# Two more attention units turned by DMA transposes on a shared ring, and the mixed tiles' scores on quarters of the array

## The chip, the core and the metric

One NeuronCore of a Trainium2 chip runs the whole program in one launch. The metric is device time in microseconds, the median of the runs. The engines are TensorE (PE; its weight loads are PEld), VectorE (DVE), ScalarE (ACT), GpSimd (POOL) and SyncE (SP), whose queue issues most of the DMAs.

## What is computed

Attention over 4 batches, 8 heads, 576 positions and a head dimension of 64, with a bias from a small network on relative positions, and then a gated product over the 2304 tokens it yields (width 512, inner width 1536):

```python
scores = 0.125 * q @ k.T + bias[None]          # bias: relu(x @ w1 + b1) @ w2, x = log1p|i-j| / log1p(max(i,1))
p = exp(scores - max(scores)); p = p / (sum(p) + 1e-9)
x = (p @ v).transpose(0, 2, 1, 3).reshape(2304, 512)
out = ((x @ w_a) * (x @ w_b)) @ w_out
```

## The kernel before

The work is 32 units `u`: for each half `c` of the query rows (`c` = 0: rows 0 to 255 of each head; `c` = 1: the other 320), each of 4 batches and each of 4 pairs of heads. A unit of the first half has four tiles of 128 query rows (`A0 B0 A1 B1`: head A or B of the pair, row block), a unit of the second half five: `A2 B2 A3 B3` and the mixed tile `T`, which holds the last 64 rows of both heads, head A in partitions 0 to 63 and head B in 64 to 127. The 144 tiles are numbered by `n`; units 0 to 15 hold tiles 0 to 63 (`N0` = 16 a batch), units 16 to 31 tiles 64 to 143 (`N1` = 20 a batch).

`attn_steps` runs a loop over `n`. In step `n` the bias rows of tile `n+2` are loaded on SP's queue; `soft1(n)` lets DVE add scores and bias and take the row extremum (L508) and ACT take the exponential with its sum (L513); loads and preparation of coming units follow; then PE computes the scores of tile `n+1` (`qk`); and `soft2(n-1)` normalises tile `n-1`. What happens to a normalised tile depends on `NF` = 12:

- Units below `NF`: POOL scales in float32 (L563), a step later `turn` lets PE transpose the tile in five blocks (L575) and ACT copies them out of PSUM (L585); `pv` multiplies float32 values: 5 blocks by 2 heads.
- Units from `NF` on: `split_turn` makes a high half on POOL (L543) and a low half with two DVE instructions (L545), both float16, in one tile `ph`, and one DMA transpose on SP's queue turns it into `pt` (L551). `pv` multiplies 14 products by 2 heads in float16, with V split in two halves by ACT and DVE in `prep_v` (L439, L440). Their `pv` comes one step later than that of the units before.

Rings: the exponentials `p` have 3 buffers; `ph` has 2 in the pool `yp`, and 2 more in the pool of the second half for odd tiles beyond 64. PSUM has one buffer `qk` for scores and one buffer `tp` for the turned blocks; from tile 51 on, odd tiles' scores use `tp`, so that scores have two buffers. V of units below `NF` is loaded into the `vs` ring, V of the others into the ring `rv` of 2, which `v_scale` (the size of the next batch's V, begun at tiles 12, 28 and 38) uses as well.

Scores of units from 8 on use q and k each split in two float32r halves (`prep_k`, `prep_q`). An ordinary tile takes 4 products; `T` takes 8, with a tile `qt` of q's last 64 columns of both heads, padded by zeros from POOL (L422) and filled by ACT and DVE (L426, L427).

PE's order is written by hand: `merge` deals out steps of the gated product (`moe_main`, lines 702 to 758), of the weights' conversion and of the attention in fixed proportions; `LEADS` says how many tiles into the next batch a batch's product begins. The other engines are ordered by a scheduler. At the start `first_units` computes 16 units of the bias table through a ring `bo` of 6, each written to DRAM from POOL's queue (L174); the other 20 follow between tiles 48 and 61.

Of the kernel before, what the change touches and what calls it, by code (L numbers as in the profile page):

```python
# [47 lines left out]
NF = 3 * NP  # L48
# [4 lines left out]
def attention_moe(ctx, tc, q0d, q1d, kd, vd, idn, wp, wa, wb, wo, lsw, lg, rl, out):  # L53
# [10 lines left out]
    xt, cpool, epool, xpool, ypool = [], [None], [None], [None], [None]  # L64
# [210 lines left out]
    w16, wos, gpool = {}, {}, [None]  # L275
# [93 lines left out]
    def load_unit(u):  # L369
        b, hp, c = UNITS[u]  # L370
        n = TOK + TAIL * c
# [18 lines left out]
        else:  # L390
            rk = att.tile([128, S], F32, tag="rk", name="rk", bufs=1)
            rq = att.tile([128, 2, n], F32, tag="rq", name="rq", bufs=1)
            with paced():
                nc.sync.dma_start(out=rk, in_=kd[b, hp])
                nc.sync.dma_start(out=rq, in_=(q1d if c else q0d)[b, hp])
# [15 lines left out]
    def prep_q(u):  # L411
        b, hp, c = UNITS[u]
        rq = st["raw", u][1]
        if u < 2 * NP:
            st["qs", u] = rq
            return
        dst = att.tile([128, 2, 2 * TOK], F32R, tag="qs", name="qs", bufs=2)
        segs = [(dst.rearrange("p c (h n) -> p c h n", h=2), rq[:, :, 0:TOK])]
        if c:

            qt = xpool[0].tile([128, 2, 4, TAIL], F32R, tag="qt", name="qt", bufs=2)
            nc.gpsimd.memset(qt[:, :, 1:3].bitcast(F32), 0.0)  # L422
            segs.append((qt[:, :, ::3], rq[:, :, TOK:]))
            st["qt", u] = qt.rearrange("p c (h x) n -> p c h (x n)", h=2)
        for d, s in segs:
            nc.scalar.copy(d[:, 0], s)  # L426
            nc.vector.tensor_tensor(out=d[:, 1], in0=s, in1=d[:, 0].bitcast(F32), op=ALU.subtract)  # L427
        st["qs", u] = dst
# [31 lines left out]
    def qk(n):  # L460
        u, t = TILES[n]
        pool, tag = (tpp, "tp") if n > 3 * N0 + 2 and n % 2 else (qkp, "qk")
        ps = pool.tile([128, 2, 512], F32, tag=tag, name="qk", bufs=1)
        q, k = st["qs", u], st["ks", u]
# [7 lines left out]
        elif t == "T":  # L472
            prods = [(st["qt", u][:, p, j], k[:, j]) for p in range(2) for j in range(2)]
        else:
            j = int(t[0] == "B")
            c0 = TOK * j + 128 * (int(t[1]) % 2)
            prods = [(q[:, p, c0:c0 + 128], k[:, j]) for p in range(2)]
# [59 lines left out]
    def split_turn(n, p, rc):  # L537
# [3 lines left out]
        pool = cpool[0] if n > B * N0 and n % 2 else ypool[0]  # L541
        ph = pool.tile([128, 2 * S], F16, tag="ph", name="ph", bufs=2)
# [82 lines left out]
    def attn_steps():  # L625
        vgen = [None]
        for n in range(NT + 4):
# [11 lines left out]
            for ahead, un in ((a, TILES[n + a][0]) for a in (6, 4, 3, 1, 0) if n + a < NT and FIRST[TILES[n + a][0]] == n + a):  # L639
# [11 lines left out]
                elif ahead == int(un < NF):  # L651
# [16 lines left out]
            if n >= 3 * N0 + 4 and (n - 3 >= NT or TILES[n - 4][0] != TILES[n - 3][0]):  # L668
                pv(TILES[n - 4][0], pvp)
            if n == B * N0 + 1:  # L670
                chunk_pool(1)
            if n >= 2 and n - 2 < 3 * N0:
# [6 lines left out]
            elif N0 + 3 <= n < 3 * N0 + 3 and TILES[n - 3][0] != TILES[n - 2][0]:  # L679
# [8 lines left out]
    def moe_block(xs, rows, mps, vi, spill=False):  # L688
# [7 lines left out]
        for f in range(FC):  # L696
# [20 lines left out]
            else:  # L717
                gs.append(g_parts(g))
# [84 lines left out]
    LEADS = [3, 4, 4, 5] + [8] * 4  # L803
# [11 lines left out]
    with tc.tile_pool(name="bg", bufs=1, side="right") as bg, tc.tile_pool(name="eq", bufs=1, space=PSUM) as eq, \  # L815
# [21 lines left out]
        def first_units(banks):  # L837
            for un in range(NU0):
# [3 lines left out]
                bias_unit(bh, lambda: banks(un), un, hs, 6, nc.gpsimd)  # L842
# [63 lines left out]
    wstack.close()  # L906
    with tc.tile_pool(name="bg2", bufs=1, reuse_waits="tile") as bg:
# [5 lines left out]
        ypool[0] = ctx.enter_context(tc.tile_pool(name="yp", bufs=1, side="right", reuse_waits="tile"))  # L913
# [66 lines left out]
```

## Time and profile before

| | |
|---|---|
| Time, median of 3 runs | 760.75 us (758.56 to 760.82) |
| The profiled execution: its time, its span | 758.25 us, 756.4 us |
| PE busy, PEld busy | 703.1 us (93%), 541.8 us (72%) |
| DVE, ACT, POOL busy | 506.8 us (67%), 448.5 us (59%), 338.3 us (45%) |
| HBM read, written | 96.44 MB, 17.18 MB |
[...]

The profile gives busy time and share of the span for each engine, the costliest groups of instructions with what ended the idle time before them, and the DMA issues with their time to landing. A busy PE is not PE at its peak: matmuls are pipelined, so in a timeline the distance from one block's start to the next one's is what a block costs. The stages by tile: the reduction of tile 0 starts at 36.5 us, of tile 40 at 195.2, of tile 48 at 235.4, of tile 64 at 332.4, of tile 143 at 625.7; after that only the products remain.

### The profile page before, as it was taken

The page shows a single profiled execution, that of the slowest core. Times are in us where ns is not written, and L with a number is a line of the kernel's source. Part 1 is how long each engine was busy: PE and PEld are TensorE (multiplying, and loading weights), DVE is VectorE, ACT ScalarE, POOL GpSimd, SP SyncE. Part 2 cuts the span into 40 slices and gives each one's busy share as a digit, 9 for nine tenths or more (in the row PEclk, how much of TensorE's full clock was granted, in tenths as well). Part 3 has the DMA queues.
Part 4 walks back from the last instruction along what each step waited for, and adds up shares of the span by engine and source line. Part 5 has one row for each costly group of instructions (what it writes and reads, how often), then busy time and mean ns, then how long its engine had stood idle before and what let it go on. Part 6 is the DMA issues. An engine that isn't in the chain of part 4 may idle for free.

```text
span 756.4 us, 15529 instructions
## 1 busy us (share of the span) xinstructions
PE 703.1 (93%) x5451; PEld 541.8 (72%) x5451; DVE 506.8 (67%) x1220; ACT 448.5 (59%) x1021; POOL 338.3 (45%) x493
## 2 busy tenths in 40 slices
PE   6777898899899999998999999999999999999997
PEld 1245465678776565687877788788878877888886
DVE  7777688859986588666898888878987762110100
ACT  6878787878866687744655656556644553321310
POOL 3337667856773133223655445535543543411200
PEclk9999999999999999999999999999999999999999
DMA  8999676587745888888999999899899954000001
GB/s 257 315 367 297 221 227 201 160 263 254 257 120 149 222 188 187 212 184 195 214 265 214 248 243 210 200 263 241 202 210 253 178 119 126 11 1 29 2 14 42
DMA packets 167154, 142.96 MB, mean 189 GB/s; under 512 B 120228, under 2 KB 125092, under 8 KB 167076
## 3 DMA queue, kind: packets, MB, share of 16 engines
q1 hardware_dynamic: 159920, 126.20, 64.1%
q10 hardware_dynamic: 5876, 10.93, 5.2%
q0 software_dynamic: 1280, 4.84, 1.9%
q8 instruction: 43, 0.70, 0.4%
q14 instruction: 35, 0.29, 0.1%
HBM read 96.44 MB, written 17.18 MB: 150 GB/s over the span
## 4 chain that ended last, share of the span: by engine, by line
PE 33%; DVE 22%; issue 16%; ACT 11%; POOL 9%; DMA 7%; SPq 0%; DVEq 0%; POOLq 0%; ACTq 0%
PE ab L702 12%; PE o L751 10%; DVE p L508 5%; DVE ph L545 4%; POOL ph L543 4%; DMA bias<-bias_d 4%; ACT p L513 3%; PE psta L153 3%; POOL gl L727 2%; DVE ks L408 2%; PE pv L603 2%; DMA pt<-ph 2%; PE qk L480 2%; DVE wt L270 1%; DVE qs L427 1%
## 5 line engine op out<-in xcount | busy, mean ns | idle before, releaser
L702 PEld LDWEIGHTS <-w16t 128*128 128x128 f16 x2592 | 247.5, 98 | 47.7 <-issue 15.8
L702 PE MATMUL ab<-x,w16t 128*128 128x256 f16 x2304 | 271.1, 274 | 4.1 <-DVE g L712 2.0
L513 ACT ACTIVATE p<-p,mn 128x576 f32<-128x576 f32 x144 | 111.7, 776 | 138.6 <-DVE mn L508 127.6
L727 POOL TENSOR_TENSOR gl<-g,gh 128x256 fp32r<-128x256 f32 x96 | 79.4, 827 | 93.6 <-ACT gh L726 91.9
L751 PE MATMUL o<-wos,gh 128*128 128x512 f32 x384 | 120.8, 395 | 0.0
L557 POOL TENSOR_SCALAR sm<-sm 128x1 f32<-128x1 f32 x144 | 42.2, 293 | 168.5 <-ACT p L513 164.3
L545 DVE SCALAR_TENSOR_TENSOR ph<-p,sm,ph 128x64 f16<-128x64 f32 x192 | 100.3, 562 | 22.8 <-POOL ph L543 22.1
L508 DVE CUSTOM_DVE_ANT_0 p<-qk,bias 128x576 f32<-128x576 f32 x144 | 107.3, 748 | 12.0 <-PE tp L575 4.1
L543 POOL TENSOR_SCALAR ph<-p,sm 128x576 f16<-128x576 f32 x96 | 82.4, 858 | 49.4 <-DVE sm L558 37.4
L712 DVE SCALAR_TENSOR_TENSOR g<-ab,wv,asb 128x256 f32<-128x256 f32 x84 | 40.2, 479 | 71.5 <-ACT asb L710 71.2
L480 PE MATMUL qk<-ks,qs 128*128 128x288 f32 x384 | 73.0, 312 | 13.8 <-DVE mn L508 13.8
L751 PEld LDWEIGHTS o<-wos,gh 128*128 128x128 f32 x384 | 69.4, 188 | 16.3 <-issue 3.3
L480 PEld LDWEIGHTS qk<-ks,qs 128*128 128x128 f32 x384 | 55.8, 188 | 27.4 <-DVE mn L508 18.7
L751 PE MATMUL o<-wos,gl 128*128 128x512 f32 x192 | 75.0, 391 | 0.0
L726 ACT CAST gh<-g 128x256 fp32r<-128x256 f32 x96 | 38.4, 400 | 34.6 <-DVE g L712 34.4
L563 POOL TENSOR_SCALAR p<-p,sm 128x576 f32<-128x576 f32 x48 | 44.5, 927 | 26.6 <-DVE sm L558 18.3
L710 ACT ACTIVATE asb<-ab,wv 128x256 f32<-128x256 f32 x84 | 39.4, 469 | 28.3 <-PE ab L702 28.0
L558 DVE RECIPROCAL sm<-sm 128x1 f32<-128x1 f32 x144 | 23.0, 160 | 47.0 <-POOL sm L557 44.8
L408 DVE TENSOR_TENSOR ks<-rk,ks 64x576 fp32r<-64x576 f32 x48 | 45.8, 954 | 5.7 <-ACT ks L407 4.1
L751 PEld LDWEIGHTS o<-wos,gl 128*128 128x128 f32 x192 | 36.0, 188 | 7.9
L575 PE MATMUL tp<-idn,p 128*128 128x128 f32 x240 | 36.0, 281 | 5.0 <-ACT ptf L580 3.6
L603 PE MATMUL pv<-pt,vs 128*64 128x320 f16 (+1 forms) x560 | 40.4, 295 | 0.0
(105 smaller groups left out, 986.2 us busy)
## 6 DMA issues: line engine op xcount, KB each, us to landing
bias<-bias_d SPq DMA_DIRECT2D x128, 288.0 KB, 3.7
rv<-vd SPq DMA_DIRECT2D x32, 320.0 KB, 3.9
rk<-kd SPq DMA_DIRECT2D x24, 288.0 KB, 3.3
wraw<-wa SPq DMA_DIRECT2D x12, 512.0 KB, 6.6
wraw<-wb SPq DMA_DIRECT2D x12, 512.0 KB, 5.5
wraw<-wo SPq DMA_DIRECT2D x12, 512.0 KB, 4.3
bias_d<-bo ACTq DMA_DIRECT2D x20, 295.5 KB, 3.7
rq<-q1d SPq DMA_DIRECT2D x16, 320.0 KB, 4.1
```

The costliest lines, as they stand in the source:

```text
L408: nc.vector.tensor_tensor(out=ks[ol, j], in0=rk[sl], in1=ks[sl, j].bitcast(F32), op=ALU.subtract)
L480: nc.tensor.matmul(ps[:, hf, :HB], a, b[:, hf * HB:hf * HB + HB], start=(x == 0), stop=(x == len(prods) - 1))
L508: ttr = nc.vector.tensor_tensor_reduce(out=p.rearrange("p (a n) -> p a n", a=2), in0=ps[:, :, :HB], in1=bt.rearrange("p (a n) -> p a n", a=2),
L513: exps.append(nc.scalar.activation(p, p, AF.Exp, bias=mn, scale=-1.0, accum_out=sm))
L543: nc.gpsimd.tensor_scalar(out=ph[:, :S], in0=p, scalar1=rc, scalar2=1.0, op0=ALU.mult, op1=ALU.mult)
L545: ins = nc.vector.scalar_tensor_tensor(out=ph[:, o:o + c1 - c0], in0=p[:, c0:c1], scalar=rc, in1=ph[:, c0:c1], op0=ALU.mult, op1=ALU.subtract,
L557: nc.gpsimd.tensor_scalar(out=sm, in0=sm, scalar1=1e-9, scalar2=1.0 / (PS if u >= NF else 1.0), op0=ALU.add, op1=ALU.mult)
L563: nc.gpsimd.tensor_scalar(out=p, in0=p, scalar1=rc, scalar2=1.0, op0=ALU.mult, op1=ALU.mult)
L603: nc.tensor.matmul(ps[64 * j:64 * j + 64, o:o + N], v[:, j, :], p[:, j * N:j * N + N], start=(x == 0), stop=(x == len(prods) - 1),)
L702: nc.tensor.matmul(ab[:, j], w16[nm, f][:, pw, kk, :], xs[px][:, kk, :], start=(x % (3 * KC) == 0), stop=(x % (3 * KC) == 3 * KC - 1),)
L727: nc.gpsimd.tensor_tensor(out=gl, in0=g, in1=gh.bitcast(F32), op=ALU.subtract)
L751: nc.tensor.matmul(o, g[:, sl], wos[f][:, p], start=(f == 0 and x == 0), stop=(f == FC - 1 and x == 2))
```

## The change

Units 10 and 11 (`NF` = 10) join those that are turned by DMA; the odd tiles' second score buffer, the shift of `pv` by a step and V's split follow (`NT0` = 40 takes the place of 48). The pool `yp` goes: `ph` is drawn from the ring of `p`, which has 4 buffers instead of 3; odd tiles beyond 64 keep their own `ph` buffers. `T` takes four products in plain float32, each of 64 rows by 64 columns of the array, from a `kt` tile loaded once more from DRAM (two DMAs) and a `qt` tile loaded by its own DMA; the zero padding and the splits for `T` go. `prep_v` of the second half comes a step earlier. The ring `bo` has 5 buffers instead of 6, the third of `LEADS` is 5 instead of 4, and the last of the twelve `gh`/`gl` pairs lies in a pool of its own.

```diff
-NF = 3 * NP
+NF = 2 * NP + 2
+NT0 = 4 * NF
@@ load_unit
-            rq = att.tile([128, 2, n], F32, tag="rq", name="rq", bufs=1)
+            rq = att.tile([128, 2, TOK], F32, tag="rq", name="rq", bufs=1)
             with paced():
                 nc.sync.dma_start(out=rk, in_=kd[b, hp])
-                nc.sync.dma_start(out=rq, in_=(q1d if c else q0d)[b, hp])
+                nc.sync.dma_start(out=rq, in_=(q1d if c else q0d)[b, hp, :, :, 0:TOK])
@@ prep_q
-        segs = [(dst.rearrange("p c (h n) -> p c h n", h=2), rq[:, :, 0:TOK])]
-        if c:
-
-            qt = xpool[0].tile([128, 2, 4, TAIL], F32R, tag="qt", name="qt", bufs=2)
-            nc.gpsimd.memset(qt[:, :, 1:3].bitcast(F32), 0.0)
-            segs.append((qt[:, :, ::3], rq[:, :, TOK:]))
-            st["qt", u] = qt.rearrange("p c (h x) n -> p c h (x n)", h=2)
-        for d, s in segs:
-            nc.scalar.copy(d[:, 0], s)
-            nc.vector.tensor_tensor(out=d[:, 1], in0=s, in1=d[:, 0].bitcast(F32), op=ALU.subtract)
+        d, s = dst.rearrange("p c (h n) -> p c h n", h=2), rq[:, :, 0:TOK]
+        nc.scalar.copy(d[:, 0], s)
+        nc.vector.tensor_tensor(out=d[:, 1], in0=s, in1=d[:, 0].bitcast(F32), op=ALU.subtract)
         st["qs", u] = dst
+
+    def load_kt(u):
+        b, hp, _ = UNITS[u]
+        kt = xpool[0].tile([128, 2, HB], F32, tag="kt", name="kt", bufs=1)
+        for hf in range(2):
+            src = kd[b, hp, :, hf * HB:hf * HB + HB].rearrange("(j d) n -> d j n", j=2)
+            nc.sync.dma_start(out=kt[64 * hf:64 * hf + 64], in_=src)
+        qt = xpool[0].tile([128, 2, TAIL], F32, tag="qt", name="qt", bufs=2)
+        nc.sync.dma_start(out=qt, in_=q1d[b, hp, :, :, TOK:])
+        st["kt", u], st["qt", u] = kt, qt
@@ qk
-        pool, tag = (tpp, "tp") if n > 3 * N0 + 2 and n % 2 else (qkp, "qk")
+        pool, tag = (tpp, "tp") if n > NT0 + 2 and n % 2 else (qkp, "qk")
+        if t == "T":
+            q, k = st.pop(("qt", u)), st.pop(("kt", u))
+            for j in range(2):
+                for hf in range(2):
+                    sl = slice(64 * hf, 64 * hf + 64)
+                    nc.tensor.matmul(
+                        ps[64 * j:64 * j + 64, hf, :HB], q[sl, j, :], k[sl, j, :], start=True, stop=True
+                    )
+            st["qk", n] = ps
+            return
-        elif t == "T":
-            prods = [(st["qt", u][:, p, j], k[:, j]) for p in range(2) for j in range(2)]
@@ soft1
-        pool, bufs = att, 3
-        p = pool.tile([128, S], F32, tag="p", name="p", bufs=bufs)
+        p = att.tile([128, S], F32, tag="p", name="p", bufs=4)
@@ split_turn
-        pool = cpool[0] if n > B * N0 and n % 2 else ypool[0]
-        ph = pool.tile([128, 2 * S], F16, tag="ph", name="ph", bufs=2)
+        if n > B * N0 and n % 2:
+            ph = cpool[0].tile([128, 2 * S], F16, tag="ph", name="ph", bufs=2)
+        else:
+            ph = att.tile([128, 2 * S], F16, tag="p", name="ph", bufs=4)
@@ attn_steps
-            for ahead, un in ((a, TILES[n + a][0]) for a in (6, 4, 3, 1, 0) if n + a < NT and FIRST[TILES[n + a][0]] == n + a):
+            for ahead, un in ((a, TILES[n + a][0]) for a in (6, 4, 3, 1, 0, -1) if 0 <= n + a < NT and FIRST[TILES[n + a][0]] == n + a):
-                elif ahead == int(un < NF):
+                elif ahead == -1:
+                    if UNITS[un][2]:
+                        load_kt(un)
+                elif ahead == int(not NF <= un < B * NP):
-            if n >= 3 * N0 + 4 and (n - 3 >= NT or TILES[n - 4][0] != TILES[n - 3][0]):
+            if n >= NT0 + 4 and (n - 3 >= NT or TILES[n - 4][0] != TILES[n - 3][0]):
-            if n >= 2 and n - 2 < 3 * N0:
+            if n >= 2 and n - 2 < NT0:
                 turn(n - 2, tpp)
@@ the products and the start
-    LEADS = [3, 4, 4, 5] + [8] * 4
+    LEADS = [3, 4, 5, 5] + [8] * 4
-                bias_unit(bh, lambda: banks(un), un, hs, 6, nc.gpsimd)
+                bias_unit(bh, lambda: banks(un), un, hs, 5, nc.gpsimd)
...
```

## Rows read from the trace of the kernel before

**Rows 1.** Windows: stretch, length, busy us (x count), clock, DMA share, GB/s.

```profile
195.00:235.00 40.00, 36.69 (x294) 29.93 (x295) 32.04 (x73) 29.52 (x65) 26.39 (x32) 1.00 0.55 174
235.00:344.00 109.00, 105.50 (x798) 72.33 (x797) 75.07 (x175) 74.58 (x162) 29.28 (x49) 1.00 0.80 189
344.00:416.00 72.00, 65.82 (x547) 54.92 (x547) 60.60 (x147) 40.78 (x97) 38.01 (x57) 1.00 0.97 225
416.00:488.00 72.00, 69.24 (x565) 58.73 (x565) 62.22 (x146) 43.28 (x104) 34.90 (x57) 1.00 1.01 230
```

**Rows 2.** PE's timeline (start, length, line, block): a mixed tile's scores, then pv.

```profile
430.92 1.32 PE L480 MATMUL qk<-ks,qt 128*128 128x288 f32 x8 [0.51 <-DVE mn L508]
432.17 2.09 PE L603 MATMUL pv<-pt,vs 128*64 128x320 f16 x28
```

**Rows 3.** PE's timeline: float32 on two row groups, and on four column groups.

```profile
61.18 1.24 PE L494 MATMUL qk<-rkf,rqf 64*128 64x288 f32 x8
62.35 0.77 PE L575 MATMUL tp<-idn,p 128*128 128x128 f32 x5
...
239.45 0.74 PE L153 MATMUL psta<-h,w2s 128*32 128x320 f32 x8
240.12 0.80 PE L480 MATMUL qk<-ks,qs 128*128 128x288 f32 x4
...
310.47 1.24 PE L153 MATMUL psta<-h,w2s 128*32 128x288 f32 x16
311.65 2.79 PE L702 MATMUL ab<-x,w16t 128*128 128x256 f16 x24
```

**Rows 4.** PE's timeline: a turned tile, pv in float32, pv in float16.

```profile
205.93 0.71 PE L575 MATMUL tp<-idn,p 128*128 128x128 f32 x5
206.56 2.53 PE L603 MATMUL pv<-ptw,rvw 128*64 128x256 f32 x20
209.02 1.48 PE L702 MATMUL ab<-x,w16t 128*128 128x256 f16 x12
...
286.74 1.72 PE L603 MATMUL pv<-pt,vs 128*64 128x256 f16 x28
288.39 1.49 PE L702 MATMUL ab<-x,w16t 128*128 128x256 f16 x12
```

**Rows 5.** DVE's timeline: reductions of tiles 40, 48, 68; a pair of low halves.

```profile
195.23 0.75 DVE L508 CUSTOM_DVE_ANT_0 p<-qk,bias 128x576 f32<-128x576 f32 x1
...
235.43 0.76 DVE L508 CUSTOM_DVE_ANT_0 p<-qk,bias 128x576 f32<-128x576 f32 x1 [1.85 <-PE tp L575]
...
328.39 0.95 DVE L545 SCALAR_TENSOR_TENSOR ph<-p,sm,ph 128x64 f16<-128x64 f32 x2
...
349.59 0.74 DVE L508 CUSTOM_DVE_ANT_0 p<-qk,bias 128x576 f32<-128x576 f32 x1
```

**Rows 6.** Groups by shape: busy us, mean ns, idle before: the low half of V.

```profile
L440 DVE SCALAR_TENSOR_TENSOR vs<-rv,vs,vs 128x640 f16<-128x640 f32 x20 | 23.2, 1161 | 4.0 <-ACT vs L439 3.8
```

**Rows 7.** Waits, 180 to 240 us: total us, times, longest.

```profile
PEld qk L480 <- DVE mn L508: 6.6, 6, 2.8
```

**Rows 8.** DMA, 416 to 488 us: packets, MB, share of queue q1; issues, median us to landing.

```profile
q1 hardware_dynamic: 29215, 15.96, 98.7%
...
bias<-bias_d SPq DMA_DIRECT2D x17, 288.0 KB, 3.5
...
pt<-ph SPq DMA_TRANSPOSE x20, 4.1
```

**Rows 9.** SP's timeline: the first DMA transposes of the second half.

```profile
350.79 8.56 SPq L551 DMA_TRANSPOSE pt<-ph  x5
```

**Rows 10.** The tile `bo`, 0 to 40 us: its DMA issues, landing min/median/max.

```profile
L174 POOL DMA_DIRECT2D bias_d<-bo x16: 530/556/4220, 9.5 to 34.8; - x16
...
DMA to landing us min/median/max: 3.1/6.2/10.4
```

**Rows 11.** Waits, whole run: reductions that waited for PE's turning.

```profile
DVE p L508 <- PE tp L575: 4.1, 5, 1.9
```

More of the change, by code (lines that the diff above doesn't have):

```diff
@@ L63, in attention_moe @@
     winv = cst.tile([128, FC, 2], F32, name="winv")
-    xt, cpool, epool, xpool, ypool = [], [None], [None], [None], [None]
+    xt, cpool, epool, xpool = [], [None], [None], [None]
     vsc = []
@@ L273, in w_unit @@
         return t.bitcast(F32)
-    w16, wos, gpool = {}, {}, [None]
+    w16, wos, gpool = {}, {}, [None, None]
     w16t = cst.tile([128, FC, 2, 2, KC, 128], F16, name="w16t")
@@ L370, in load_unit @@
         b, hp, c = UNITS[u]
-        n = TOK + TAIL * c
         if u < 2 * NP:
@@ L678, in attn_steps @@
                     pv_first(n - 3, pvp)
-            elif N0 + 3 <= n < 3 * N0 + 3 and TILES[n - 3][0] != TILES[n - 2][0]:
+            elif N0 + 3 <= n < NT0 + 3 and TILES[n - 3][0] != TILES[n - 2][0]:
                 pv(TILES[n - 3][0], pvp)
@@ L717, in moe_block @@
             else:
-                gs.append(g_parts(g))
+                gs.append(g_parts(g, f))
             yield
@@ L721, in moe_block, with g_parts @@
             yield from moe_out(gs, rows, mps)
-    def g_parts(g):
-        gh = gpool[0].tile([128, TOK], F32R, tag="gh", name="gh", bufs=FC)
-        gl = gpool[0].tile([128, TOK], F32R, tag="gl", name="gl", bufs=FC)
+    def g_parts(g, f):
+        pool, bufs = (gpool[0], FC - 1) if f < FC - 1 else (gpool[1], 1)
+        gh = pool.tile([128, TOK], F32R, tag="gh", name="gh", bufs=bufs)
+        gl = pool.tile([128, TOK], F32R, tag="gl", name="gl", bufs=bufs)
         nc.scalar.copy(gh, g)
@@ L906, in attention_moe @@
     wstack.close()
+    gpool[1] = ctx.enter_context(tc.tile_pool(name="gq", bufs=1, side="right", reuse_waits="tile"))
     with tc.tile_pool(name="bg2", bufs=1, reuse_waits="tile") as bg:
@@ L912, in attention_moe @@
         stream[1] = [2 * first + 2 * nst * i // nb for i in range(nb)]
-        ypool[0] = ctx.enter_context(tc.tile_pool(name="yp", bufs=1, side="right", reuse_waits="tile"))
         merge((main, 2 * FC - 22 + GS + 1), (asteps, n2 - n2 * 5 // 8))
```

## The prediction

> **What bounds the kernel now.** I read the windows by stage first, then PE's timeline inside them, then the waits, then the DMA view. In the windows [rows 1] PE is busy for 36.7 of 40 us where tiles 40 to 47 run, 105.5 of 109 in the stage after that, and 65.8 and 69.2 of 72 in the first two batches of the second half; the second half repeats at 72 us a batch. So PE is the first bound nearly everywhere, with 3 to 6 us of idle a stage, and work taken from it should shorten the kernel unless something else is close. Two things are. In the stretch from 195 to 235 DVE is busy for 32.0 of 40 us, and in the second half the DMA share is 0.97 to 1.01 [rows 1], 98.7% of it one queue [rows 8]. These two decide how much of PE's gain reaches the end.
>
> **The mixed tiles' scores.** Today a `T` takes eight products; from its start to the start of the next block it is 432.17 - 430.92 = 1.25 us [rows 2]. After the change it is four products in float32 on 64 rows by 64 columns. A float32 product shows as two matmuls in the trace (the four products of a pair of tiles are x8 in [rows 3]), so eight matmuls of 288 columns stand against eight. No row shows four quarters of the array at work at once. The bounds come from the two packings that the trace has, both float32 and 288 columns. Two row groups: eight matmuls in 62.35 - 61.18 = 1.17 us. Four column groups: sixteen in 311.65 - 310.47 = 1.18 us, so 0.59 for eight [rows 3]. If quarters pack like two groups only, a `T` saves 0.08 us; if like four, 0.66. I take 0.65 us for the new `T`, near the row of four groups, because a quarter differs from its neighbour by rows or by columns, and each of these is seen to overlap. That saves 0.60 us for each of 16 tiles: 9.6 us of PE time, 2.4 a batch, bounds 1.3 and 10.6.
>
> The switch between shapes is a cost to look at, since each `T` now stands between blocks of other shapes. By the rows, a block of sixteen costs 1.18 us and a lone block of eight at 320 columns 240.12 - 239.45 = 0.67 us [rows 3]; with a time t for eight at 288 and a fixed part s, 2t + s = 1.18 and 1.11t + s = 0.67 give t = 0.57 and s = 0.03 us, so 16 switches cost half a us. [...]
>
> What `T` adds is transfers: per unit two halves of `kt` (288 KB together) and `qt`, 64 KB that `rq` loses. By bytes that is 4 x 0.295 = 1.2 MB on 15.96 MB a batch [rows 8], 7.4%. `kt` is issued in the step after the unit's first tile and read by PE for the scores of the fifth, so it has about two steps, 72 / 20 = 3.6 us each, against 3.5 us to land for a bias load [rows 8]. Behind these issues on SP's queue stand bias loads and transposes. DVE, ACT and POOL lose the small instructions that filled `qt`; none is a bound, so I count them at nothing.
>
> How much of 2.4 us a batch arrives? PE idles 2.8 us of 72 today [rows 1], DVE is at 62 of 72, so there is room for a 70 us batch. I take six tenths: -6 us over four batches. Ends: -9.6 with everything passed on, 0 if the DMA or the pairs eat it.
>
> **Units 10 and 11.** PE loses eight turned tiles, 206.56 - 205.93 = 0.63 us each: 5.0 us. The `pv` goes from 209.02 - 206.56 = 2.46 to 288.39 - 286.74 = 1.65 us [rows 4], twice: 1.6 us. Eight more tiles have two score buffers, and PE's weight loads wait 6.6 us for the single one between 180 and 240 [rows 7], of which some half lies there. So if PE set the pace, 6.6 us and a little more would go.
>
> DVE pays: eight pairs of low halves at 0.95 us [rows 5] are 7.6 us, two low halves of V at 1.16 us [rows 6] are 2.3: 9.9 us on a stretch in which it has 8.0 us free of 40 [rows 1]. The reductions of tiles 40 and 48 stand 235.43 - 195.23 = 40.2 us apart [rows 5]. DVE would need 32 + 9.9 = 41.9, at some 95% busy 44 us: 4 longer than now. But the load is uneven: the conversion of the output weights, which shares DVE, ends before the stretch does, and the last two or three of the eight pairs fall into the next stage, where DVE is at 75 of 109 and PE's saving counts in full. Of the 6.6 us I therefore put about half, 3.3, where PE is the bound, and of DVE's 9.9 us about half, with the gaps left there filled, as 4.3 us of lengthening. Net +1 us; ends -8 (PE alone) and +5 (DVE alone, with 1.4 us of product that the longer third lead moves out of a stretch where PE would be idle: 1/17 of the some 24 us of products that PE's 36.7 us leave beside turning, scores and `pv`).
>
> On SP's queue eight transposes of about 1.7 us each (five in 8.56 us [rows 9]) come in, and bias loads stand behind them, two tiles ahead, that is two steps of 5 us against 3.5 us to land [rows 8]: hidden here, since the DMA share is 0.55 [rows 1]. V of units 10 and 11 now takes slots of the ring that sizes the next batch's V from tile 38 on; one of those loads may wait for `prep_v` of unit 10. Its result is read at tile 48, some steps later; I count nothing, up to 3 us if PE's small product for it comes late in PE's fixed order.
>
> **One ring for `p` and `ph`.** Up to tile 64 the four slots alternate, so `p` has two and `ph` two. A slot of `p` is used again two tiles later, after the low halves of its tile; at 5 us a step that is covered. Beyond 64 a slot of an even `ph` passes to the `p` four tiles later, so a reduction on DVE waits for a transposing transfer, and PE waits behind that reduction for its score buffer. Before, the waiting step was POOL's high half. In the steady part the transfer is issued about two steps before and lands in 4.1 us [rows 8]: covered with a margin of some 2 us. At the change of halves it is not: the first five transposes leave only at 350.79 [rows 9] and the first lands near 354.9, while the reduction of tile 68, which would take that slot, ran at 349.59 [rows 5]. That is up to 5.3 us late, or nothing if the transfer is sent earlier. I take +1.5, once. On tiles below 40 the fourth `p` buffer can win back the 4.1 us in which reductions waited for PE's turning [rows 11]; most of that was not PE's bound; I take -1.
>
> **The start.** `bo` with five buffers instead of six: the 16 stores are issued (34.8 - 9.5) / 15 = 1.7 us apart, and land 6.2 us (median), at worst 10.4, later [rows 10]. Five buffers cover 8.4 us, which the median passes and the worst does not. I take +1, ends 0 and +3. The `gh`/`gl` pools and the earlier `prep_v` cost nothing: each buffer has the same use before it.
>
> **The sum.** -6 (mixed tiles) + 1 (units 10, 11) + 1.5 (ring) - 1 (fourth `p`) + 1 (start) = -3.5 us on the profiled execution's 758.25, that is 754.8. That execution lies 2.5 us under the median of the runs; on 760.75 the same sum gives 757.2, and I say 757.
>
> **The rivals.**
> A. PE sets the pace throughout: -9.6 - 6.6 + 1.5 = -14.7, 746 us. For it: PE's busy time [rows 1]. Against it: DVE's 41.9 us in 40.
> B. The quarters pack only in pairs: -1.3 for all `T`, +1 + 1.5 + 0 for the rest: 762 us, no change. For it: the only row with row groups gives 1.17 us. The change then does not do what it says.
> C. DVE becomes the bound of the 195 to 235 stretch, +5, the change of halves costs its +5, and `T` brings only half, -3; with the start's +1: 769 us. It decides once DVE has no idle time left between the reductions of tiles 40 and 48, and they stand over 45 us apart.
> D. The DMA engines become the bound of the second half: 7.4% more bytes at a share of 1.01 make 72 us into 77; less the 1 us of slack, +4 a batch and +16 in all: 777 us instead of a gain. For it: the share. Against it: bias loads still land in 3.5 us there [rows 8], which a saturated queue would not do. It decides once a batch of the second half takes more than 72.3 us.
>
> **How the numbers follow.** A measurement of this kernel can tell about 0.3%, 2.3 us. My forecast has a chance of 0.45, with its own range 752 to 758; A 0.15, B 0.18, C 0.13, D 0.09. Faster is the forecast and A, 0.60; B is no change, 0.18; C and D are slower, 0.22. A range of 747 to 768 leaves out D and part of A and of C, some 2 in 10.
>
> **What would show it.** `T` from its start to the next block at 0.6 to 0.7 us (1.2 speaks for B). A batch of the second half at 70 to 71 us. The reductions of tiles 40 and 48 some 40 to 42 us apart, with DVE nearly without idle time between them. A DVE or PE wait for `pt<-ph` near the change of halves of 2 us or so. The mixed tiles' PE waiting for `kt`, or bias loads that take 5 us to land, would make the prediction wrong on the slow side; two score buffers that let DVE and PE both run without gaps from tile 40 on, on the fast side.

## The result, and the profile after

The changed kernel takes 765.78 us (median of 12 runs, 763.24 to 771.19) against 760.64 (12 runs beside them): a ratio of 1.0065 [1.0045, 1.0086]. It is slower by 5 us where 3.5 us less were forecast. The profiled execution has 763.58 us (span 761.8 us, mean granted clock 0.984 of full speed) against 758.25 (756.4, 0.995).

The windows by stage, as in [rows 1] (stretch, length, busy us of each engine with its count, granted clock, DMA share, GB/s):

```profile
195.00:235.00 40.00, 31.86 (x249) 25.08 (x248) 38.15 (x78) 26.98 (x59) 29.89 (x28) 0.96 0.78 209
235.00:344.00 109.00, 105.05 (x813) 72.77 (x812) 81.48 (x191) 75.62 (x165) 35.21 (x54) 0.97 0.87 205
344.00:416.00 72.00, 63.01 (x540) 51.68 (x539) 57.17 (x136) 39.85 (x91) 31.91 (x50) 0.98 1.04 227
416.00:488.00 72.00, 66.06 (x558) 54.42 (x558) 57.18 (x136) 39.41 (x92) 32.13 (x50) 1.00 1.13 242
488.00:560.00 72.00, 68.61 (x570) 56.17 (x569) 58.77 (x140) 41.08 (x95) 33.15 (x53) 1.00 1.10 242
```

PE is busy for less time everywhere: 66.06 of 72 us from 416 to 488, where before had 69.24. The time did not get shorter; PE got idle. What rose is the DMA share: 1.13 against 1.01 there, 0.78 against 0.55 from 195 to 235. In that first stretch DVE now is busy for 38.15 of 40 us and PE for 31.86: the two have changed places. The granted clock fell too, to 0.96 and 0.97 in the first two stretches, which had 1.00 before.

The mixed tile did what was forecast. PE's timeline of the changed kernel, answering [rows 2]:

```profile
421.32 0.71 PE L472 MATMUL qk<-kt,qt 64*64 64x288 f32 x8 [0.70 <-DVE ks L408]
421.97 2.09 PE L615 MATMUL pv<-pt,vs 128*64 128x320 f16 x28
```

421.97 - 421.32 = 0.65 us from block to block, where it was 1.25. But a batch of 20 tiles did not become shorter. DVE's timeline, the reductions of tiles 40, 48, 88, 108 and 128 in the changed kernel:

```profile
196.42 0.74 DVE L518 CUSTOM_DVE_ANT_0 p<-qk,bias 128x576 f32<-128x576 f32 x1
...
237.93 0.76 DVE L518 CUSTOM_DVE_ANT_0 p<-qk,bias 128x576 f32<-128x576 f32 x1 [0.19 <-issue]
...
424.02 0.74 DVE L518 CUSTOM_DVE_ANT_0 p<-qk,bias 128x576 f32<-128x576 f32 x1
...
497.64 0.76 DVE L518 CUSTOM_DVE_ANT_0 p<-qk,bias 128x576 f32<-128x576 f32 x1
...
570.15 0.74 DVE L518 CUSTOM_DVE_ANT_0 p<-qk,bias 128x576 f32<-128x576 f32 x1
```

and of tiles 88, 108 and 128 in the kernel before:

```profile
420.97 0.75 DVE L508 CUSTOM_DVE_ANT_0 p<-qk,bias 128x576 f32<-128x576 f32 x1
...
491.39 0.74 DVE L508 CUSTOM_DVE_ANT_0 p<-qk,bias 128x576 f32<-128x576 f32 x1
...
563.73 0.74 DVE L508 CUSTOM_DVE_ANT_0 p<-qk,bias 128x576 f32<-128x576 f32 x1
```

Two batches took 73.6 and 72.5 us, and 70.4 and 72.3 before. Tiles 40 to 48 took 41.5 us, 1.3 more than the 40.2 of [rows 5].

The starts of the reductions split the whole span into stages (us):

| Stage | Before | Changed | Difference |
|---|---|---|---|
| Start to tile 0 | 36.5 | 38.1 | +1.6 |
| Tiles 0 to 40 | 158.7 | 158.3 | -0.4 |
| Tiles 40 to 48 | 40.2 | 41.5 | +1.3 |
| Tiles 48 to 64 | 97.0 | 98.9 | +1.9 |
| Tiles 64 to 72 (change of halves) | 31.6 | 30.3 | -1.3 |
| Tiles 72 to 143 | 261.7 | 261.7 | 0.0 |
| Tile 143 to the end | 130.7 | 132.9 | +2.2 |

So the second half did not get longer; it failed to get shorter, where the forecast had its 6 us. What the profiled execution lost stands ahead of tile 64 and behind tile 143. Of the 4.5 us that are lost by tile 64, 3.2 lie between tiles 40 and 64, where units 10 and 11 now are turned by transfers.

In that stretch stands a wait that the forecast does not have. SP's queue, DVE and PE in the changed kernel:

```profile
237.80 1.61 SPq L563 DMA_TRANSPOSE pt<-ph  x1
239.50 0.53 SPq L125 DMA_DIRECT2D u<-lsw  x1
```

```profile
236.79 0.95 DVE L557 SCALAR_TENSOR_TENSOR ph<-p,sm,ph 128x64 f16<-128x64 f32 x2
...
243.53 0.98 DVE L144 TENSOR_SCALAR h<-u,lgs 128x320 f32<-128x320 f32 x3
```

```profile
244.06 1.78 PE L154 MATMUL psta<-h,w2s 128*32 128x320 f32 x8 [3.60 <-DVE h L144]
```

and SP's queue before:

```profile
227.93 0.42 SPq L124 DMA_DIRECT2D u<-lsw  x1
```

The load `u` (the positions' logarithms) starts the bias table's other 20 units; `h` is the small network's inner layer, `psta` its product on PE. It leaves 11.6 us later than before, right behind a transpose that had itself waited for DVE's low half (236.79 + 0.95 = 237.74). DVE therefore makes `h` late, and PE, whose order is fixed, idles for 3.60 us. Then the granted clock falls; the windows from 240 us on:

```profile
240.00:244.00 4.00, 0.46 (x3) 0.04 (x1) 3.32 (x7) 1.14 (x3) 3.02 (x4) 0.87 1.10 262
244.00:248.00 4.00, 3.94 (x15) 2.59 (x16) 2.03 (x7) 1.87 (x5) 0.00 (x0) 0.50 0.48 110
```

At 0.50 the same block of eight takes 1.78 us instead of 0.74 [rows 3].

At the change of halves three timelines of the changed kernel tell one story: DVE's reduction of tile 68 (349.59 in [rows 5]), PE's next scores, and SP's queue:

```profile
358.18 0.76 DVE L518 CUSTOM_DVE_ANT_0 p<-qk,bias 128x576 f32<-128x576 f32 x1 [4.64 <-DMA pt<-ph]
```

```profile
359.09 1.30 PE L491 MATMUL qk<-ks,qs 128*128 128x288 f32 x4 [4.71 <-DVE mn L518]
```

```profile
350.99 1.29 SPq L428 DMA_DIRECT2D kt<-kd  x2
352.33 0.60 SPq L430 DMA_DIRECT2D qt<-q1d  x1
353.04 8.11 SPq L563 DMA_TRANSPOSE pt<-ph  x4
```

The reduction needs the ring slot of an even `ph`, and that slot is free once its transposing transfer has landed. The transposes leave at 353.04, behind the loads of `kt` and `qt`; before, the first left at 350.79 [rows 9]. DVE idles for 4.64 us and PE for 4.71 behind it. Tile 68 is 8.6 us later than before, tile 72 (367.2 us against 364.0) only 3.2. Tile 64 was 4.5 us late already, so by tile 72 the wait is made up.

The same waits come back in the steady part. Waits of the changed kernel from 366 to 626 us (total us, times, longest):

```profile
POOL ph L555 <- DMA pt<-ph: 19.6, 8, 3.6
...
DVE p L518 <- DMA pt<-ph: 4.5, 3, 2.7
...
PE pv L615 <- DMA pt<-ph: 2.6, 3, 1.7
...
PE qk L472 <- DMA kt<-kd: 2.5, 1, 2.5
```

None of these four has a row in that stretch of before. Its DMA view from 416 to 488 us, answering [rows 8]:

```profile
q1 hardware_dynamic: 31138, 16.80, 110.1%
...
bias<-bias_d SPq DMA_DIRECT2D x15, 288.0 KB, 4.0
...
kt<-kd SPq DMA_DIRECT2D x8, 144.0 KB, 4.6
...
pt<-ph SPq DMA_TRANSPOSE x20, 4.7
```

5.3% more bytes, but 11.6% more packet time (110.1 against 98.7). Bias loads land in 4.0 us instead of 3.5, transposes in 4.7 instead of 4.1. Over two batches, 416 to 560 us, it is 3.6 against 3.5 for the bias loads and 4.6 against 3.9 for the transposes.

### The profile page after: what moved, and what is told of

Read it like the earlier page. It is cut to its first block, busy times and chain, and to the rows that moved or that the text cites. A ratio compares the mean times of both kernels' runs of the same rounds, so it can differ in the third digit from the quotient of the medians.

```text
span 761.8 us, 15513 instructions
## 1 busy us (share of the span) xinstructions
PE 695.1 (91%) x5427; PEld 528.4 (69%) x5427; DVE 510.0 (67%) x1222; ACT 443.4 (58%) x999; POOL 339.1 (45%) x477
## 4 chain that ended last, share of the span: by engine, by line
PE 44%; DVE 16%; DMA 12%; issue 12%; ACT 7%; POOL 7%; SPq 2%; ACTq 0%; DVEq 0%; POOLq 0%
PE ab L717 17%; PE o L767 14%; DMA pt<-ph 6%; DVE p L518 3%; PE qk L491 3%; PE psta L154 3%; POOL ph L555 3%; DVE ph L557 3%; PE pv L615 2%; DMA bias<-bias_d 2%; ACT p L523 2%; POOL gl L743 2%; DVE ks L408 2%; PE pv L535 1%; DVE w16t L268 1%
## 5 line engine op out<-in xcount | busy, mean ns | idle before, releaser
L557 DVE SCALAR_TENSOR_TENSOR ph<-p,sm,ph 128x64 f16<-128x64 f32 x208 | 107.3, 556 | 33.1 <-POOL ph L555 31.9
L569 POOL TENSOR_SCALAR sm<-sm 128x1 f32<-128x1 f32 x144 | 47.1, 327 | 167.5 <-ACT p L523 162.2
L743 POOL TENSOR_TENSOR gl<-g,gh 128x256 fp32r<-128x256 f32 x96 | 76.3, 795 | 96.8 <-ACT gh L742 94.0
L555 POOL TENSOR_SCALAR ph<-p,sm 128x576 f16<-128x576 f32 x104 | 92.1, 886 | 59.1 <-DVE sm L570 33.7
L727 DVE SCALAR_TENSOR_TENSOR g<-ab,wv,asb 128x256 f32<-128x256 f32 x84 | 40.2, 478 | 69.8 <-ACT asb L725 69.5
L725 ACT ACTIVATE asb<-ab,wv 128x256 f32<-128x256 f32 x84 | 39.4, 469 | 30.3 <-PE ab L717 29.9
L615 PE MATMUL pv<-pt,vs 128*64 128x320 f16 (+1 forms) x616 | 43.8, 293 | 2.6 <-DMA pt<-ph 2.6
L575 POOL TENSOR_SCALAR p<-p,sm 128x576 f32<-128x576 f32 x40 | 35.8, 895 | 18.0 <-DVE sm L570 15.4
L615 PEld LDWEIGHTS <-vs 128*64 128x64 f16 x616 | 33.1, 110 | 15.0 <-issue 8.6
```

The source lines that it names most:

```text
L555: nc.gpsimd.tensor_scalar(out=ph[:, :S], in0=p, scalar1=rc, scalar2=1.0, op0=ALU.mult, op1=ALU.mult)
L557: ins = nc.vector.scalar_tensor_tensor(out=ph[:, o:o + c1 - c0], in0=p[:, c0:c1], scalar=rc, in1=ph[:, c0:c1], op0=ALU.mult, op1=ALU.subtract,
L569: nc.gpsimd.tensor_scalar(out=sm, in0=sm, scalar1=1e-9, scalar2=1.0 / (PS if u >= NF else 1.0), op0=ALU.add, op1=ALU.mult)
L615: nc.tensor.matmul(ps[64 * j:64 * j + 64, o:o + N], v[:, j, :], p[:, j * N:j * N + N], start=(x == 0), stop=(x == len(prods) - 1),)
L727: nc.vector.scalar_tensor_tensor(out=g, in0=ab[:, 1], scalar=wv[:, f, 1:2], in1=asb, op0=ALU.mult, op1=ALU.mult)
L743: nc.gpsimd.tensor_tensor(out=gl, in0=g, in1=gh.bitcast(F32), op=ALU.subtract)
```

## The experiments

All ratios are to the kernel before, run on the same chip beside them. The medians of before were 759.97, 760.66, 760.83, 761.12 and 761.77 us on the five chips used below. Where stages of a variant are given, they come from its one profiled execution, between the starts of the reductions as in the table above.

### The change taken apart

**`t_only`**: the kernel before with the mixed tiles' part alone (`kt` and `qt` loaded, four products on the quarters).

> The kernel before with the mixed tiles' scores on quarters alone (kt and qt loaded, no splits for T); units 10 and 11, the rings and the leads as before. Theory R (the shared ring costs what T saves): T's 0.6 us x 16 arrives, 751 to 755 us against 760.6 of before. Theory L (the added loads eat T's gain, because the DMA engines are near their limit in the second half): 759 to 763 us, with a DMA share above 1.05 in 416 to 488 and transposes that land later than 4.1 us.

763.26 us, 1.0036 [1.0012, 1.0060]. PE waits for `kt` three times in the second half, 4.6 us in all.

**`turn_only`**: the changed kernel with `T` as before, so the turning, the ring and the start alone (q's tail comes by a DMA of its own).

> The changed kernel with T's scores as before (eight products, zero padding, no kt; the tail of q by its own DMA): units 10 and 11 by transposes, the shared ring, the leads, five bo buffers. Theory R: this part carries the loss, 766 to 771 us (765.8 of the changed kernel plus up to 0.6 x 16 = 9.6 of T's gain less what does not arrive), with the reduction of tile 68 waiting some 4 us for a transpose. Theory L: no added loads, 760 to 763 us.

762.09 us, 1.0024 [1.0006, 1.0042]. The two parts add up to the 0.65% of the change, and each alone costs time: there is no bad meeting of two good parts. The trace of `turn_only` has its loss ahead of tile 64 (4.6 us later than before, with the same wait of 3.59 us for `h`); behind it, it gains 4.0 us.

**`t_diag`**: as `t_only`, but `T` reads the raw `k` that is loaded anyway, from the quarter on the diagonal where it lies, two quarters at a time; no `kt`.

```diff
-            for j in range(2):
-                for hf in range(2):
-                    sl = slice(64 * hf, 64 * hf + 64)
-                    nc.tensor.matmul(ps[64 * j:64 * j + 64, hf, :HB], q[sl, j, :], k[sl, j, :], ...)
+            for x in range(2):
+                for j in range(2):
+                    hf, sl = (x + j) % 2, slice(64 * j, 64 * j + 64)
+                    nc.tensor.matmul(ps[sl, hf, :HB], q[sl, j, :], k[sl, hf * HB:hf * HB + HB], ...)
```

> The kernel before with T in float32 from the raw k that is there already: each head on its own quarter of the diagonal, two at a time, so no kt load (qt is loaded by its own DMA; raw k gets a second buffer). T costs PE about 1.0 us instead of 0.65. Theory L: no added loads, so what PE saves arrives: 16 x 0.25 = 4, 756 to 758 us, and not slower than T on four quarters with its loads. Theory R: slower than T on four quarters by 0.35 x 16 = 5.6 us.

756.68 us, 0.9951 [0.9922, 0.9979]. PE's timeline shows what `T` costs here, 615.71 - 614.60 = 1.11 us:

```profile
614.60 1.19 PE L483 MATMUL qk<-rkx,qt 64*64 64x288 f32 x8
615.71 2.09 PE L625 MATMUL pv<-pt,vs 128*64 128x320 f16 x28
```

A `T` that costs PE 0.46 us more than the change's makes the kernel 0.85% faster than the change's `T`. So what the second load brings with it outweighs what PE's shorter `T` saves.

**`own_ring`**: the changed kernel, with even `ph` from tile 64 on in two buffers of their own.

```diff
-            ph = att.tile([128, 2 * S], F16, tag="p", name="ph", bufs=4)
+            pool, tag, bufs = (xpool[0], "ph", 2) if n >= B * N0 else (att, "p", 4)
+            ph = pool.tile([128, 2 * S], F16, tag=tag, name="ph", bufs=bufs)
```

> The changed kernel with the even ph from tile 64 on in two buffers of their own again, so that no exponential waits for a transpose there; the rest unchanged. Theory R: the wait of 4.6 us of the reduction of tile 68 and the 11.1 us in all go: 757 to 761 us. Theory L: the stall goes but the second half stays at 72 us a batch: 762 to 764 us.

759.62 us, 1.0002 [0.9979, 1.0024]: 0.6%, some 5 us, come back. Between 366 and 626 us its waits have no row with `pt<-ph` at all.

### Putting the good parts together, and the start

**`after_diag`** is the changed kernel with `t_diag`'s `T`; **`diag_own`** is that with `own_ring`'s buffers.

> The changed kernel with T on the diagonal quarters from raw k and no kt loads; shared ring, units 10 and 11 and the rest as changed. If the parts add up (t_diag -3.3, turning with the shared ring +2.1): 758 to 760 us. If the shared ring costs less once the loads are gone: 755 to 757 us.

756.65 us, 0.9933 [0.9909, 0.9958].

> The same with the even ph from tile 64 on in two buffers of their own. Theory R (the ring's stall is what turning units 10 and 11 pays): the 6 us that own buffers gave the changed kernel come off, 752 to 755 us, under t_diag's 756.7. Rival D (DVE bounds the stretch of tiles 40 to 47, so turning two more units by transfers gains nothing): 756 to 759 us.

756.81 us, 0.9938 [0.9915, 0.9961]. With one load of `k` the shared ring costs nothing that can be measured. Its waits are not gone. Waits of `after_diag`, 366 to 626 us:

```profile
POOL ph L556 <- DMA pt<-ph: 14.4, 7, 3.5
...
DVE p L519 <- DMA pt<-ph: 1.8, 1, 1.8
```

They are smaller, and the transposes land in 4.0 us (416 to 560 us) instead of 4.6 in the changed kernel. At the change of halves the transposes leave earlier, with no `kt` ahead of them:

```profile
348.10 0.55 SPq L399 DMA_DIRECT2D rk<-kd  x1
348.70 0.58 SPq L431 DMA_DIRECT2D qt<-q1d  x1
349.39 7.59 SPq L564 DMA_TRANSPOSE pt<-ph  x4
```

Tile 68 is 4.5 us late here, and tile 72 1.1 us ahead of before. Against `t_diag` (0.9951), turning units 10 and 11 is worth 0.1 to 0.2%, within the intervals.

The trace shows where the shared ring costs. From tile 64 to 72 it costs nothing: 30.3 us in the changed kernel, 32.6 in `own_ring`. From tile 72 to the end it is 394.6 against 388.8. With one whole load of `k` the two are alike there, 389.3 in `after_diag` and 389.1 in `diag_own`.

**`bo5`**: the kernel before with the ring `bo` of 5.

> The kernel before with five bo buffers instead of six, nothing else. If the start's wait for the bias table's stores reaches the end: 761 to 763 us; if the later slack takes it up: 759 to 761 us, within noise of before.

761.56 us, 1.0000 [0.9978, 1.0022]: the start costs nothing that can be measured, but 1 us could not be seen in this interval.

### Is it SP's queue?

**`diag_kt`** (`t_diag` with `kt` loaded as well and read by nothing), **`diag_kt_quarter`** (a quarter of its columns) and **`diag_kt_act`** (issued from ACT's queue) were meant as the price of the load alone.

> T on the diagonal quarters from raw k, as in t_diag (756.7 us), and beside it the two kt loads of each unit of the second half into a tile that nothing reads. Theory L (the loads slow the other transfers): 760 to 763 us, transposes landing later than the 4.2 us of t_diag. Rival W (only PE's own waits for kt cost, 4.6 us in the trace of T alone): the loads cost nothing where nobody waits for them, 756 to 758 us.

770.82 us, 1.0131 [1.0101, 1.0162].

> diag_kt (T on the diagonal quarters, two kt loads a unit that nothing reads) with a quarter of the columns in each load: as many DMAs, as many rows, a quarter of the bytes. Theory Q (the place and time in SP's queue is what a load costs): about as slow as diag_kt, 767 to 771 us. Theory E (the DMA engines' time for the bytes is what it costs): about a quarter of the 14 us between t_diag and diag_kt, 758 to 762 us.

768.09 us, 1.0105 [1.0084, 1.0125].

> diag_kt with the two unread kt loads issued from ACT's queue instead of SP's; same bytes. Theory Q: most of the 14 us go, 757 to 761 us (ACT pays some 0.6 us an issue and has time). Theory E: they stay, 767 to 772 us.

784.61 us, 1.0341 [1.0302, 1.0379]. The first and the third lie outside every range forecast for them, and all three are inconclusive. A tile that nobody reads is free at once, so its loads are sent in a bunch: from 331.4 to 500.1 us in `diag_kt`, 327.2 to 483.5 and 328.3 to 408.8 in the others, instead of one pair with each unit up to 610. They price a blocked queue, not a load in its place. An issue of these loads took 0.61 us on ACT's queue in `diag_kt_act` and 0.63 on SP's in `diag_kt` (medians of 32).

**`t_only_act`** and **`own_act`**: `t_only` and `own_ring` with the two `kt` loads issued from ACT's queue.

```diff
-            nc.sync.dma_start(out=kt[64 * hf:64 * hf + 64], in_=src)
+            nc.scalar.dma_start(out=kt[64 * hf:64 * hf + 64], in_=src)
```

> The kernel before with T on four quarters, the kt loads from ACT's queue. Theory Q: T's PE time arrives, 752 to 756 us (t_only 763.3). Theory E: as t_only, 761 to 765 us.

762.81 us, 1.0025 [1.0004, 1.0046], within the interval of `t_only`. From 416 to 560 us (packets, MB, share) its load is split over two queues, and the transposes land no earlier (4.4 us in `t_only`):

```profile
q1 hardware_dynamic: 60097, 31.17, 99.0%
q10 hardware_dynamic: 2880, 3.41, 8.3%
...
pt<-ph SPq DMA_TRANSPOSE x41, 4.9
```

> The changed kernel with the even ph from tile 64 on in buffers of their own and the kt loads from ACT's queue: a candidate for a version faster than both. Theory Q: 751 to 756 us. Theory E: as own_ring, 758 to 761 us.

761.79 us, 1.0019 [0.9997, 1.0041]. So moving the loads to another queue wins nothing as a whole. By stage there is more to it. From tile 48 to 72 the runs with ACT's queue are the shorter ones, 128.6 us against 129.9 (`t_only_act`, `t_only`) and 127.9 against 131.3 (`own_act`, `own_ring`); from tile 72 to the end they are the longer ones, 393.9 against 392.0 and 393.5 against 388.8. So the place on SP's queue may well cost at the change of halves; whether ACT's own delay or the engines' time takes it back later is not separated. PE's waits for `kt` (rival W) are not the whole of it either: `t_only_act` and `own_act` have none in the second half.

### The load, its form, and PE's time

**`four_t`** keeps the change's `T` (0.65 us) without a second load: the raw `k` of the second half is loaded once, by the two DMAs of `kt`, and the splits for the other tiles are made from it. **`four_turn`** is the changed kernel with that, **`four_own`** is `four_turn` with `own_ring`'s buffers.

```diff
-                nc.sync.dma_start(out=rk, in_=kd[b, hp])
+                for hf in range(2):
+                    src = kd[b, hp, :, hf * HB:hf * HB + HB].rearrange("(j d) n -> d j n", j=2)
+                    nc.sync.dma_start(out=rk[64 * hf:64 * hf + 64], in_=src)
```

> The kernel before with T on four quarters and no byte loaded twice: raw k of the second half comes once, already in the order that T needs (two DMAs of half the rows' length), and the splits for the other tiles are made from it. T costs PE 0.65 us as in the change. Theory E (the loads of k for a second time ate T's gain): faster than t_diag by most of 16 x 0.45 = 7 us, 750 to 754 us. Rival P (PE's time for T is not what the second half waits for; t_diag was faster for the splits that it drops): like t_diag, 755 to 758 us. Rival D2 (it is the number of DMAs or their shorter rows): like t_only, 761 to 765 us.

758.90 us, 0.9988 [0.9965, 1.0012], between the ranges of P and D2.

> The changed kernel with k of the second half loaded once in T's order (no second load); shared ring, units 10 and 11 turned by transfers, leads, as changed. Theory E: the 765.8 of the changed kernel lose the loads' whole price, 750 to 755 us. Rival P: as after_diag, 756 to 758 us. Rival D2: 763 to 767 us.

764.48 us, 1.0044 [1.0024, 1.0065].

> The same with the even ph from tile 64 on in two buffers of their own. If the ring costs only while the loads are there (after_diag and diag_own were alike): within 1 us of four_turn. If the shared ring costs by itself: 3 to 5 us under four_turn.

759.46 us, 0.9982 [0.9960, 1.0004]. Dropping the second load gains about 0.5% (`t_only` to `four_t`); the shared ring costs 0.6% again (`four_turn` against `four_own`). But with the faster `T` and the same bytes, `four_t` is no faster than `t_diag`. Three runs on `t_diag` narrow down why.

**`diag_split`**: `t_diag`, its `k` loaded by two DMAs, one for each half of the columns, into all 128 partitions: as many rows of 1152 bytes as in `four_t`.

```diff
-                nc.sync.dma_start(out=rk, in_=kd[b, hp])
+                for hf in range(2):
+                    hb = slice(hf * HB, hf * HB + HB)
+                    nc.sync.dma_start(out=rk[:, hb], in_=kd[b, hp, :, hb])
```

> t_diag, with the raw k of each mixed unit loaded by two DMAs, one for each half of the columns: the same bytes once, but 256 rows of 1152 bytes in place of 128 of 2304, as four_t has them. T stays on the diagonal quarters at 1.11 us. Theory E2 (what four_t lost against t_diag, 758.90 to 756.68, lies in the shorter rows and the additional DMA): ratio 0.998 to 1.000, DMA share of 416 to 488 us at 1.06 or more. Rival P (rows and count of DMAs cost nothing; four_t is no faster since T's time on TensorE isn't what its second half waits for): 0.994 to 0.996, share about 1.03.

756.38 us, 0.9936 [0.9904, 0.9968]: as `t_diag`. Neither shorter rows nor a second DMA cost anything that can be measured.

**`diag_load`**: `t_diag`, with `T`'s `k` loaded a second time by one DMA into 128 partitions, and read by `T`.

```diff
+        kt = xpool[0].tile([128, S], F32, tag="kt", name="kt", bufs=1)
+        nc.sync.dma_start(out=kt, in_=kd[b, hp])
```

> t_diag, with T's k loaded a second time, as in t_only, but by one DMA with rows of 2304 bytes into a buffer of its own, and read by T: 288 KB more for each of the mixed units, in time with its tile. It is the price of the second load with a reader. Theory D (the second load takes what T gives back): ratio 0.999 to 1.002, DMA share of 416 to 488 us 1.08 to 1.12, the second half 3 to 5 us longer than in t_diag. Rival: only the two DMAs with rows of 1152 bytes cost: 0.994 to 0.996, share at most 1.06.

760.98 us, 0.9994 [0.9972, 1.0017]: a second load in its place, with a reader, costs 0.4% against `t_diag`, 0.6% against `diag_split`.

**`diag_twice`**: `t_diag` with the matmuls of each `T` issued twice.

```diff
-            for x in range(2):
+            for x in range(4):
```

> t_diag, with the matmuls of each T issued twice, the second time over the first's result: 1.11 us more of TensorE for each of 16 tiles, 17.8 us in all, and no byte more to move. Theory PE (in the second half TensorE's time reaches the end wherever the DMA engines leave it): t_diag has 7 us of idle TensorE in 344 to 622 us (270.7 of 278 busy), so 756.7 + 11 to 18 = 767.5 to 774.5, ratio 1.009 to 1.018. Rival P (TensorE isn't what the second half waits for): at most 3 us, 0.995 to 0.999.

772.61 us, 1.0150 [1.0116, 1.0185]: 16 us over `diag_split` on the same chip for 17.8 us of PE, so nine tenths arrive. With no byte added, time added on PE reaches the end. That time taken from PE below `t_diag`'s does so as well is not shown: no run with a `T` of 0.65 us is faster than `t_diag`. The windows of `t_diag` from 488 on agree: PE is idle for 1.5 us of 134.

```profile
488.00:560.00 72.00, 70.49 (x570) 57.35 (x569) 60.65 (x143) 40.54 (x94) 33.39 (x53) 1.00 1.04 227
560.00:622.00 62.00, 62.00 (x508) 51.48 (x507) 48.47 (x110) 32.00 (x77) 28.32 (x45) 1.00 0.89 186
```

`diag_split` and `four_t` move the same bytes in the same rows and number of DMAs, but in `four_t` each DMA writes 64 partitions instead of 128. Two more things differ: `T`'s time on PE, and the buffers of raw `k`, three at the change of halves in `diag_split` and two in `four_t`. The DMA views from 416 to 560 us (packets, MB, share of q1; KB each, us to landing), in turn of before, `diag_split`, `four_t`, `diag_load` and `t_only`:

```profile
q1 hardware_dynamic: 57517, 31.45, 95.7%
```

```profile
q1 hardware_dynamic: 61572, 31.53, 98.7%
...
rkx<-kd SPq DMA_DIRECT2D x16, 144.0 KB, 3.9
```

```profile
q1 hardware_dynamic: 62878, 31.80, 103.8%
...
rk<-kd SPq DMA_DIRECT2D x8, 144.0 KB, 4.0
rkx<-kd SPq DMA_DIRECT2D x8, 144.0 KB, 4.8
```

```profile
q1 hardware_dynamic: 62171, 33.77, 104.1%
...
kt<-kd SPq DMA_DIRECT2D x8, 288.0 KB, 5.1
```

```profile
q1 hardware_dynamic: 62366, 33.63, 111.5%
...
kt<-kd SPq DMA_DIRECT2D x16, 144.0 KB, 4.8
```

Two pairs differ in the form of the load, in `T`'s time on PE and, the first, in those buffers: `diag_split` to `four_t` (+5.1 points of share, +0.5% of time) and `diag_load` to `t_only` (+7.4 points, +0.4%). Two pairs differ by the second load: `diag_split` to `diag_load` (+5.4 points, +0.6%) and `four_t` to `t_only` (+7.7 points, +0.5%). In these pairs the time rises with the packet time of the DMA engines, also where the bytes are the same. And the +0.4 to 0.5% for the form is net: `T`'s 0.46 us less, 7.4 us in all, lie on the other side of it.

That the packet time is the cause is argued, not shown, and other traces speak against it as the only one. `diag_own` and `four_own` have the same buffers and differ by the form of the load and `T`'s time: +0.4% of time, but 104.3% and 104.6% of share. By stage, the trace of `four_own` is longer from tile 48 to 72 (130.5 us against 127.9) and not behind it (388.8 against 389.1 to the end); `four_t` and `diag_split` show the same, 130.2 against 127.5 and then 390.4 against 390.5. So most of the difference lies at the change of halves, where the clock differs too (0.95 from 344 to 416 us in `four_t`, 1.00 in `diag_split`); behind it `T`'s shorter time brings nothing. There a load of `k` stands ahead of the first transposes of the second half on SP's queue, and they leave 18.7 us after tile 64's reduction in `four_own`, 17.0 us in `diag_own`. The runs do not separate the destination from that place in the queue.

## Why the prediction was wrong, point by point

**The mixed tiles on PE** were right: 0.65 us forecast, 0.65 measured. B (pairs only) is out.

**How much arrives** is the step that failed. Six tenths of 9.6 us were to arrive, -6; the part by itself measured +0.36%, some +3 us. I took the missing four tenths for a guess about PE's idle time and DVE. PE's share was not the weak place: with no byte added some nine tenths of added time arrive (`diag_twice`). What has no term in my sum is the price of the second load, and it took the gain and more: without it the same `T` is 0.5% faster (`four_t` against `t_only`), and a second load in `t_diag`, read in its place, costs 0.4% (`diag_load`). That is rival D's side, to which I gave 0.09, but not all of D's mechanism. Its condition, a batch over 72.3 us, tells little, as a batch of before took 72.3. My reason against it, bias loads that land in 3.5 us, does not follow either: at a share of 1.01 they landed in 3.5, and over two batches of the changed kernel in 3.6, while the transposes went from 3.9 to 4.6. D's price was wrong in both directions. Bytes (7.4%) were the wrong measure: packet time rose by 15.8 points from before to `t_only` for 6.9% more MB. And a share over 1 did not lengthen a batch in proportion: at 1.13 from 416 to 488 us, where before had 1.01, two batches took 73.6 and 72.5 us instead of 70.4 and 72.3, so D's +4 us a batch and 777 us did not come; T's part costs 3 us in all, after PE's gain. How the load's price divides into the engines' time, its place on SP's queue at the change of halves, PE's waits for `kt` and the clock stays open.

**Units 10 and 11** were right between tiles 40 and 48: +1 forecast, +1.3 measured. DVE became the bound there, as C has it, but at 38.15 of 40 us and 41.5 us apart, under C's 45. The next stage I had wrong: the pairs that fall into it were to find room, and PE's saving to count in full. Instead tiles 48 to 64 took 1.9 us more, with PE's wait of 3.60 us for `h`, held up behind DVE and SP's queue. I had looked at that queue for the bias loads and V, not for the table's load. It is no accident of one run: in all eight kernels that turn units 10 and 11 by transfers PE waits 1.9 to 3.6 us for `h` there, the clock from 235 to 290 us is 0.94 or 0.95, and tiles 40 to 64 take 139.7 to 142.6 us; in the twelve others the clock is 1.00 and they take 136.5 to 139.3. The forecast does not mention the clock. Over the whole kernel the part without the ring's cost is about -0.1% (`diag_own` against `t_diag`, `four_own` against `four_t`), up to -0.3% (`own_ring` against `t_only`).

**The ring** was right in mechanism, but mis-sized and misplaced: +1.5 once, ends 0 and 5.3, against 0.6%, some 5 us, in two pairs (the changed kernel and `own_ring`; `four_turn` and `four_own`). The wait at the change of halves came, at 4.64 us, but its delay was made up by tile 72. What I had called covered, the steady part with its "margin of some 2 us", was not: from 366 on POOL waits 19.6 us and DVE 4.5 us for landed transposes. The margin assumed transfers that land in 4.1 us; the change itself made them 4.7. With one whole load of `k` (4.0 us) the ring is free. The stages of both pairs put the cost in that steady part, 394.6 against 388.8 us and 394.7 against 388.8 from tile 72 to the end, and none at the change of halves. `turn_only`, with transposes at 4.0 us too, takes 390.1 from there; its trace loses ahead of tile 64.

**The fourth `p` buffer** (-1) was not measured by itself; tiles 0 to 40 took 0.4 us less. **The start** (+1): the trace of the changed kernel has tile 0 later by 1.6 us, and ACT waits 2.8 us for `bo`. `bo5` shows no difference at the end, within 1.7 us either way.

**The sum**: of +5 us, T's part makes about 3 and the turning with its shared ring about 2. That the time, 765.8 us, lies nearest C's 769 is chance: C's conditions did not come. `own_ring` alone brings the change back to the time of before, one load of `k` with the slower `T` to 0.7% below it. `after_diag`, `diag_own`, `diag_split` and `t_diag` (0.9933 to 0.9951) are all faster than both kernels; among them the intervals do not choose.

## What to carry to other kernels

When PE is busy for 96% of a stage and the DMA engines have a share of 1 (69.24 of 72 us and 1.01 from 416 to 488 us here), work taken from PE must not be paid in transfers: price an added load by a run that has it in its place, with a reader and in the same form, not in bytes. Here a slower operand order that reads what is already there (1.11 us) beat a faster one that needs a reload (0.65 us): 756.68 us against 763.26. A ring shared with tiles that a transfer empties inherits that transfer's landing time (4.7 us here, with 19.6 us of waits on POOL), so ask what the rest of the change does to that time. And where an engine becomes the bound of a stretch, follow what stands behind it on the queues into the next stretch: a load that leaves late there can stop an engine whose order is fixed (`u` left 11.6 us later here, and PE stood for 3.60 us).

## What the runs showed of the hardware

- Eight float32 matmuls of 288 columns took 0.65 us on four quarters of the array, made of two row groups and two column groups (the changed kernel), and 1.11 us on the two diagonal quarters, two at a time (`t_diag`).
- The same 288 KB as two transfers of 64 partitions instead of two of 128, at equal row length, stood at 103.8% against 98.7% of packet time over eight units in one pair of kernels (`four_t`, `diag_split`); `t_diag`, with one whole load, has 100.3%, and another pair (`four_own`, `diag_own`) shows 104.6% against 104.3%.
- In the changed kernel the granted clock fell behind two stretches in which PE was nearly idle: PE was busy for 0.46 us from 240 to 244, and the clock stood at 0.50 from 244 to 248; PE was busy for 0.38 us from 354 to 358, and the clock stood at 0.63 from 358 to 362. The mean clock of a run, by its median, is 0.979 in the changed kernel and 0.979 to 0.984 in all eight that turn units 10 and 11 by transfers; in the others, but for `diag_kt_act` at 0.976, it is 0.985 to 0.992. Runs of before differ along with it: 758.5 us at 0.993, 766.6 at 0.984. So the clock can be much of the 5 us; how much isn't separated here.
